# Converting staged pieces of queries, keys and values two steps behind their load, with at most four pieces staged in three steps

## The chip, the cores and the metric

The kernel runs on one core of a Trainium2 chip. The metric is the time of one execution on the device, in microseconds. Before the change the median of three runs is 926.92 us (923.02 to 928.24). TensorE is PE in the rows (PEld its weight loads), VectorE DVE, ScalarE ACT, GpSimd POOL. SyncE, SP, issues nearly all transfers, in the order of its list (SPq in the rows).

## The reference

Attention over 4 batches and 8 heads, 576 positions of 64 numbers each, where each row of scores keeps its 32 largest. Then a dense layer with a maximum over three products, and then a mixture of 8 experts, in which each of the 2304 tokens goes to one:

```python
scores = scale * np.matmul(q, k.transpose(0, 1, 3, 2))
kth = np.partition(scores, -32, axis=-1)[..., -32:-31]
scores = np.where(scores >= kth, scores, -1e9)
attn = softmax(scores); x = attn @ v              # per batch and head
h = np.maximum(np.maximum(x @ w1, x @ w2), x @ w3) @ w_out
expert = argmax(h @ w_gate); p = softmax weight of it
out[expert == e] = p * (np.maximum(h[e] @ ew1[e], 0) @ ew2[e])
```

## The kernel before

All products take float16 pairs: a number is split into a high half and a low half (the rest), and a product is three matmuls. So every operand in float32 must be split, by ACT (high half, scaled) and by DVE (scaled number less high half). For a low half ACT may first write the scaled number to a PSUM buffer (line 740) and DVE subtract from there (line 741); where PSUM buffers are scarce DVE reads the staged number itself (line 734).

The program is written out step by step, each engine's list in the order of the code; no scheduler moves anything. A loop (line 1596) counts steps `t`. One attention tile (128 query rows of a head; two half tiles are paired) enters per step, 144 in all, and its stages lie some steps apart: scores on PE (line 887), evacuation by ACT (894), searches for the 32nd largest on DVE and POOL, exponential on ACT (1046), split of the probabilities on ACT and POOL (1057, 1061), their transposition by a transfer from SP (1066), and product with the values on PE (1080). Between these stand units of the dense layer and of the experts, let in by a credit per step (`run_units`, line 1515): 36 matmuls for a unit of the dense layer, 24 for one of an expert. Where credit is left over and nothing is ready, four filler matmuls are written (1705).

Pieces of queries, keys and values (128 rows of 512 numbers, 256 KB; the last of a batch half of that) come by `preps`, a list of (due step, release step, function, which piece), sorted by due step. In a step at most one released piece begins, or two if the first is due soon. Beginning it (`prep_q`, `prep_k`, `prep_v`, lines 760 to 822) takes one of four staging tiles `st` and issues the load from SP; the function that it returns converts it. Those functions wait in `pend_p`: the conversion stands near the head of the next step, ahead of that step's evacuation on ACT. One step behind the conversion SP issues the transposing transfer of the halves (line 793 for queries), and two steps behind it the copies inside the query tile (797). The weights of one expert use the same staging tiles (`piece`, `half_piece`, lines 1306 and 1319): at most one piece a step, converted two steps behind its load (line 1331).

The 18 tiles of 128 tokens are ranked one after another: the gate product (1195), DVE's choice of an expert, two small matmuls that count tokens per expert (`unit_rank`, 1239 and 1240), and a scatter of the rows to their expert's place (1260). The first expert's tokens are worked on meanwhile, in blocks (slots): a first layer (355) and a second one of four units (366 to 368). When all 18 are ranked, DVE makes the table of the blocks that are left (lines 268 to 331), SP fills gaps (340), issues weight loads that are skipped where the right weights are there already (439, 448) and gathers the rows of the first blocks (427), and `finale` works through the list.

Of the kernel before, what the change touches and what calls it, by code (L numbers as in the profile page):

```python
# [19 lines left out]
def kernel(  # L20
# [43 lines left out]
    WARM, ST = 4, 4  # L64
# [30 lines left out]
    def attempt(ctx, general):  # L95
# [526 lines left out]
        with ExitStack() as p1:  # L622
# [43 lines left out]
            clock = [0]  # L666
# [4 lines left out]
            def after(n, fn):  # L671
                due.setdefault(clock[0] + n, []).append(fn)
# [35 lines left out]
            def stage_tile():  # L708
                if clock[0] < 0:
                    return s_p.tile([P, S], F32, tag="s", name="s")[:, 0:H * D]  # L710
                return st_p.tile([P, H * D], F32, tag="st", name="st")

            def stage_load(src, b, t):
                n = tok_rows(t)
                st = stage_tile().rearrange("p (h d) -> p h d", h=H)
                nc.sync.dma_start(out=st[0:n], in_=src[b, :, t * P:t * P + n, :].rearrange("h p d -> p h d"))
                return st
# [565 lines left out]
            ew, e1, e2, half = [], [], [], [None]  # L1283
# [16 lines left out]
            def piece_ok(i):  # L1300

                if i >= KE:
                    return bool(e2) and i < KE + 2 * KD
                return bool(picked) and clock[0] > picked + 8 and clock[0] > FREE + (0 if i < KE // 2 else L_AV + 1)

            def piece(i):

                st = stage()
                re = nc.sync.value_load(firsti[0:1, 0:1], min_val=0, max_val=NE - 1)
                if i < KE:  # L1310
                    src = ew2[bass.ds(re, 1), i * P:(i + 1) * P, :]
                    hi, lo = (w2e(e, i) for e in range(2))
                else:
                    kk, f = divmod(i - KE, 2)
                    src = ew1[bass.ds(re, 1), kk * P:(kk + 1) * P, f * 512:(f + 1) * 512]
                    hi, lo = (W1e[0][:, e, kk, f * 512:(f + 1) * 512] for e in range(2))
                return split_piece(st, src, hi, lo)

            def half_piece(kk):

                f = half[0]
                st = stage()
                re = nc.sync.value_load(firsti[0:1, 0:1], min_val=0, max_val=NE - 1)
                return split_piece(st, ew1[bass.ds(re, 1), kk * P:(kk + 1) * P, f * 512:(f + 1) * 512],
                                   W1h[0][:, 0, kk], W1h[0][:, 1, kk])
# [197 lines left out]
            for b in range(B):  # L1523
                blocks = [NQ] + list(range(NQ)) if b == B - 1 else list(range(NCH))
                start = b * (NTL // B)
                need = start
                items = []
                for t in range(NCH):
                    items.append((start - 2, start - 24, prep_k, (b, t)))
                for bi, qb in enumerate(blocks):  # L1530
                    items.append((need - 2, need - 6, prep_q, (b, qb)))
                    need += H if qb < NQ else H // 2
                for t in range(NCH):
                    items.append((start + 10, max(start - 12, 2), prep_v, (b, t)))
                preps += items
# [17 lines left out]
            with tc.manual_schedule():  # L1553
# [5 lines left out]
                def begin(it):  # L1559
                    return it[2](*it[3])  # L1560
# [5 lines left out]
                rows = lead[0], lead[1], lead[2], lead[3]  # L1566
                rest_k = lead[4:]
                clock[0] = -8
                pend_p, pend_w = [], []
                pend = [begin(it) for it in rows]  # L1570
                pend.append(begin_w())
                pend.append(begin(rest_k[0]))
# [16 lines left out]
                t = -1  # L1589
# [6 lines left out]
                while second is None or not fin() or len(ranked) < NTT:  # L1596
# [18 lines left out]
                        st_exp(n)  # L1615
                    for go in pend_p:
                        go()
                    pend_p = []
                    avail = [it for it in preps if it[1] <= t]
                    for it in avail[:2 if avail and avail[0][0] - t < 6 else 1]:  # L1620
                        preps.remove(it)
                        pend_p.append(it[2](*it[3]))
                    n = t - L_REST
                    if ok(n):
                        st_rest(n)
# [31 lines left out]
                    pend_w = []  # L1657
                    if wq:

                        for f, a in wq[:2 if t < L_KTH - 2 else 1]:  # L1660
                            wq.pop(0)
                            pend_w.append(f(*a))
                    elif not m_ps and not pend_w and t > 20:
                        p_w.close()
                        m_ps.append(p_m.enter_context(tc.tile_pool(name="mp", bufs=2, side="right")))
                        ew.append(p_m.enter_context(tc.tile_pool(name="ew", bufs=1, side="right")))
                        W1h.append(ew[0].tile([P, 2, KD, 512], F16, name="W1h"))
                    elif piece_ok(len(eld)):
                        after(2, piece(len(eld)))
                        eld.append(t)  # L1670
                    elif len(hld) < KD and half[0] is not None:
                        after(2, half_piece(len(hld)))
                        hld.append(t)
# [94 lines left out]
```

## Time and profile before

| | us |
|---|---|
| median of three runs | 926.92 (923.02 to 928.24) |
| the profiled execution | 929.35 |
| its span, first to last instruction | 927.6 |
| busy: PE / DVE / ACT / POOL | 743.9 / 746.3 / 706.1 / 596.7 |
| mean granted clock of TensorE | 0.966 of 2.4 GHz |

The terms of a sum are made against the profiled execution, and the forecast against the median. A busy share of 76 to 80% over the span is an average over three stretches with different limits, which is why the rows below go by stretch. In a row of a timeline the first two numbers are the start and the duration in us, and the bracket is the engine's idle time ahead of it with what ended it. DMA rows on SP are the time of the issue, not of the transfer.

### The profile page before, as it was taken

How to read it: one execution, taken by the hardware profiler on the slowest of the kernel's cores; microseconds unless marked ns; L12 is line 12 of the kernel's file. 1: busy time of each engine (PE TensorE's matmuls, PEld its weight loads, DVE VectorE, ACT ScalarE, POOL GpSimd, SP SyncE). 2: the span in 40 equal slices, each digit the busy share in tenths (PEclk: the TensorE clock that was granted, in tenths of full speed). 3: DMA queues.
4: the chain of work that ended last, by engine and by line, in shares of the span. 5: the costliest groups of instructions: out<-in, count | busy, mean ns of one | idle time of the engine just before them, and what ended most of it. 6: DMA issues, size and time to landing. Idle time of an engine off the chain costs nothing. (4 is left out here: it accounts for less than half of the span.)

```text
span 927.6 us, 29138 instructions
## 1 busy us (share of the span) xinstructions
PE 743.9 (80%) x10606; PEld 577.4 (62%) x10606; DVE 746.3 (80%) x3108; ACT 706.1 (76%) x1464; POOL 596.7 (64%) x554
## 2 busy tenths in 40 slices
PE   1112367889877899978988899889999999999992
PEld 0001136667665778757777688667987755687871
DVE  5999999999999899998998999998852325477660
ACT  4769899999998899898998999998861231466660
POOL 2547798898988699987877789788982221101110
PEclk9999999999899799998989999989999999999996
DMA  9863968777997798899989798878986568698370
GB/s 229 265 215 72 209 140 164 121 145 124 189 167 158 143 163 169 154 191 178 189 145 171 169 161 137 186 165 147 175 163 115 137 169 309 160 309 224 87 194 16
DMA packets 372165, 155.94 MB, mean 168 GB/s; under 512 B 331931, under 2 KB 348319, under 8 KB 372000
## 3 DMA queue, kind: packets, MB, share of 16 engines
q1 hardware_dynamic: 368128, 143.10, 75.4%
q0 software_dynamic: 3136, 9.46, 3.0%
q8 instruction: 87, 1.43, 0.7%
q10 hardware_dynamic: 736, 1.32, 0.4%
q14 instruction: 78, 0.64, 0.2%
HBM read 76.06 MB, written 16.67 MB: 100 GB/s over the span
## 5 line engine op out<-in xcount | busy, mean ns | idle before, releaser
L355 PEld LDWEIGHTS <-W 128*128 128x128 f16 x4560 | 250.9, 100 | 19.8 <-issue 16.8
L355 PE MATMUL mm<-xT,W 128*128 128x128 f16 x3456 | 215.3, 225 | 15.2 <-DVE vl L741 5.4
L968 POOL TENSOR_TENSOR f<-s,g 128x576 f32<-128x576 f32 x144 | 184.6, 1282 | 45.9 <-ACT g L962 28.2
L1061 POOL TENSOR_TENSOR phl<-e,phl 128x576 f16<-128x576 f32 x144 | 188.1, 1306 | 8.2 <-ACT phl L1057 7.4
L916 DVE MAX8 c<-s 128x8 f32<-128x96 f32 x864 | 175.1, 243 | 12.3 <-ACT s L894 8.7
L887 PEld LDWEIGHTS <-qT 128*128 128x128 f16 (+1 forms) x640 | 56.6, 107 | 191.3 <-issue 157.5
L887 PE MATMUL S<-kt,qT 128*128 128x64 f16 (+3 forms) x320 | 61.5, 342 | 109.2 <-ACT s L894 94.4
L1046 ACT ACTIVATE e<-s,be 128x576 f32<-128x576 f32 x144 | 109.8, 762 | 14.2 <-POOL phl L1061 10.3
L1080 PE MATMUL av<-vh,pt 128*128 128x65 f16 (+3 forms) x1600 | 110.7, 200 | 11.8 <-DVE xn L1129 9.8
L962 ACT ACTIVATE g<-s,bf 128x576 uint16<-128x576 f32 x144 | 111.6, 775 | 5.7
L977 DVE MAX8 vec<-f 128x8 f32<-128x576 f32 x144 | 108.7, 755 | 4.7 <-POOL f L968 1.9
L1040 POOL TENSOR_TENSOR s<-s,g 128x576 f32<-128x576 f32 x72 | 92.8, 1288 | 22.7 <-DVE e L1051 21.6
L1080 PEld LDWEIGHTS <-pt 128*128 128x128 f16 (+3 forms) x2400 | 89.4, 103 | 24.7 <-issue 11.4
L894 ACT ACTIVATE s<-S 128x576 f32<-128x576 f32 x144 | 91.7, 636 | 15.8 <-PE S L887 15.6
L1057 ACT ACTIVATE phl<-e 128x576 f16<-128x576 f32 x144 | 96.2, 668 | 7.9 <-DMA pt<-phl 7.7
L1080 PE MATMUL av<-vl,pt 128*128 128x64 f16 (+3 forms) x800 | 100.2, 197 | 0.0
L1051 DVE SCALAR_TENSOR_TENSOR e<-s,hkth,e 128x576 f32<-128x576 f32 x72 | 87.2, 1211 | 13.1 <-ACT e L1046 12.7
L456 DVE SCALAR_TENSOR_TENSOR W<-st,W 128x1024 f16<-128x1024 f32 x56 | 65.8, 1220 | 36.6 <-ACT W L455 34.5
L887 PE MATMUL S<-kT,qT 128*128 128x512 f16 (+3 forms) x320 | 48.7, 292 | 22.5 <-ACT s L894 22.5
L1164 POOL TENSOR_TENSOR hhl<-a,hhl 128x384 f16<-128x384 f32 x36 | 37.0, 1027 | 33.8 <-ACT hhl L1163 32.5
L455 ACT ACTIVATE W<-st 128x1024 f16<-128x1024 f32 x56 | 55.6, 1046 | 1.8 <-DMA xs<-zrow 1.8
L1037 ACT ACTIVATE g<-s,hkth 128x576 uint16<-128x576 f32 x72 | 54.7, 760 | 0.0
(233 smaller groups left out, 1571.2 us busy)
## 6 DMA issues: line engine op xcount, KB each, us to landing
st<-in_moe_w_dram SPq DMA_DIRECT2D x72, 512.0 KB
st<-in_moe_w_dram SPq DMA_DIRECT2D x28, 256.0 KB
raw<-in_moe_w_dram SPq DMA_DIRECT2D x12, 512.0 KB
st<-in_v_dram SPq DMA_DIRECT2D x16, 256.0 KB
hs<-he SPq DMA_DIRECT2D x16, 256.0 KB
hTe<-hs SPq DMA_DIRECT2D x8, 512.0 KB
st<-in_q_dram SPq DMA_DIRECT2D x15, 256.0 KB
qT<-qT SPq DMA_DIRECT2D x30, 128.0 KB
```

The source lines that it names most:

```text
L355: nc.tensor.matmul(out=ps[:, o * n:(o + 1) * n], lhsT=w(b, kk, c), rhs=x(a, kk), start=(kk == 0 and i == 0), stop=(kk == KD - 1 and i == 2))
L887: nc.tensor.matmul(out=ps[o:o + m, j, 0:(REM if j else NQ * P)], lhsT=qt[:, vv, hh, 0:m], rhs=kr[:, hh] if j else km[:, hh // HG, :, hh % HG],
L894: nc.scalar.activation(out=s, in_=Sps.pop(n).rearrange("p a b -> p (a b)")[:, 0:S], func=ACTF.Copy, scale=DOWN)
L916: nc.vector.max(out=c[:, i * 8:(i + 1) * 8], in_=s[:, i * CW:(i + 1) * CW])
L962: nc.scalar.activation(out=gg[n], in_=Ss[n], func=ACTF.Sign, bias=bf[g][:, i], accum_out=cnt[g][:, i])
L968: let_in(nc.gpsimd.tensor_tensor(out=ff[n], in0=Ss[n], in1=gg.pop(n).bitcast(F16), op=ALU.subtract))
L977: bulk.append(lambda: nc.vector.max(out=y8[g][:, i, 1:9], in_=y))
L1040: let_in(nc.gpsimd.tensor_tensor(out=Ss[n], in0=Ss[n], in1=zz.pop(n).bitcast(F16), op=ALU.subtract))
L1046: nc.scalar.activation(out=e, in_=Ss.pop(n) if early(n) else Ss[n], func=ACTF.Exp, scale=ESC, bias=be[g][:, i])
L1057: nc.scalar.activation(out=ph[:, 0, 0:S], in_=p, func=ACTF.Copy)
L1061: nc.gpsimd.tensor_tensor(out=ph[:, 1, 0:S], in0=p, in1=ph[:, 0, 0:S], op=ALU.subtract)
L1080: nc.tensor.matmul(out=av[o:o + m, i, 0:n], lhsT=t[0:kk, p * NCH + c, o:o + m], rhs=v_rows(x, b, c, hh)[:, 0:n], start=(c == 0 and p == 0 ...
```

## The change

A piece that is begun in step t is converted in step t+2 (`next_p` holds it for a step). Query pieces are released one step earlier, so their conversion stays in its step; pieces of keys and values convert a step later. `staged` notes the step of every staging tile that is taken, by weight pieces too, and a piece begins only while fewer than four were taken in this step and the two before it; until the pool of attention operands is closed this holds for weight pieces also.

```diff
             def stage_tile():
                 if clock[0] < 0:
                     return s_p.tile([P, S], F32, tag="s", name="s")[:, 0:H * D]
+                staged.append(clock[0])
                 return st_p.tile([P, H * D], F32, tag="st", name="st")
+
+            staged = []
+
+            def staging():
+                return sum(c > clock[0] - 3 for c in staged) < ST
...
-                    items.append((need - 2, need - 6, prep_q, (b, qb)))
+                    items.append((need - 2, need - 7, prep_q, (b, qb)))
...
                     for go in pend_p:
                         go()
-                    pend_p = []
+                    pend_p, next_p = next_p, []
                     avail = [it for it in preps if it[1] <= t]
-                    for it in avail[:2 if avail and avail[0][0] - t < 6 else 1]:
+                    for it in avail[:2 if avail and avail[0][0] - t < 7 else 1]:
+                        if not staging():
+                            break
                         preps.remove(it)
-                        pend_p.append(it[2](*it[3]))
+                        next_p.append(it[2](*it[3]))
...
+                    elif not staging() and not e1:
+                        pass
                     elif piece_ok(len(eld)):
```

Lines below the first edit stand six to ten lines lower in the changed kernel: 716 is 722 there, 1239 is 1245.

SP's list around the load of the first full query piece of the last batch (step 105 or 106). Here `qT<-qT` are the copies inside a query tile, `pt<-phl` transposes of probabilities, `xTe<-xs` a gather of an expert's rows, `mte<-xs` its small load. Before:

```order
L797 DMA qT<-qT 64x8x64 x2
L1066 DMA_TRANSPOSE pt<-phl_148 128x10x128
L1371 TENSOR_LOAD eroi
L1371 ISA x2
L1373 ISA
L1373 DMA_TRANSPOSE xTe<-xs 128x8x128
L1375 ISA
L1375 DMA mte<-xs 128x2
L716 DMA st<-in_q_dram 128x8x64
L1066 DMA_TRANSPOSE pt<-phl_149 128x10x128
```

And in the changed kernel:

```order
L722 DMA st<-in_q_dram 128x8x64
L803 DMA qT<-qT 64x8x64 x2
L1441 DMA hs<-he 128x1024
L1193 DMA_TRANSPOSE x2T<-xr 128x8x128
L1072 DMA_TRANSPOSE pt<-phl_148 128x10x128
L1072 DMA_TRANSPOSE pt<-phl_149 128x10x128
L1072 DMA_TRANSPOSE pt<-phl_150 128x10x128
L1377 TENSOR_LOAD eroi
```

The load moved from behind the gather to ahead of the copies; the gather now follows three transposes later.

PE's list around the last of the 18 rankings (`oh` is the choice of an expert, `tri` and `ones` the constant operands; `xTe` and `hTe` are a block's rows for the first and the second layer). Before:

```order
L355 LDWEIGHTS W1e
L355 MATMUL mm<-xTe,W1e 128x128
L1239 LDWEIGHTS tri_70
L1239 MATMUL mm<-oh,tri_70 128x8
L1240 LDWEIGHTS ones_69
L1240 MATMUL mm<-oh,ones_69 128x8
L366 LDWEIGHTS hTe
L366 MATMUL mm<-kt_107,hTe 128x512
```

And in the changed kernel:

```order
L368 LDWEIGHTS hTe
L368 MATMUL mm<-vh_108,hTe 128x512
L1245 LDWEIGHTS tri_70
L1245 MATMUL mm<-oh,tri_70 128x8
L1246 LDWEIGHTS ones_69
L1246 MATMUL mm<-oh,ones_69 128x8
L366 LDWEIGHTS hTe
L366 MATMUL mm<-kt_107,hTe 128x512
```

A block's second layer of 24 matmuls, which stood behind the ranking, now stands ahead of it. Its result goes out by POOL, whose list shows the blocks that follow (`xs<-xr,si` is the scatter of the ranked tile, each `ye` with `mte` one block's result, and with `mt` one of the last stage). Before:

```order
L1209 COPY xr_16330<-tok_68 128x1
L1260 DMA xs_57<-xr_16330,si_16731 19584x514
L400 DMA out_0_dram<-ye_16780,mte_92 2304x512
L400 DMA out_0_dram<-ye_17013,mte_92 2304x512
L400 DMA out_0_dram<-ye_17079,mte_92 2304x512
L400 DMA out_0_dram<-ye_17110,mte_92 2304x512
L400 DMA out_0_dram<-ye_17118,mt_16962 2304x512
```

And in the changed kernel:

```order
L1215 COPY xr_16405<-tok_68 128x1
L400 DMA out_0_dram<-ye_16766,mte_92 2304x512
L1266 DMA xs_57<-xr_16405,si_16804 19584x514
L400 DMA out_0_dram<-ye_16845,mte_92 2304x512
L400 DMA out_0_dram<-ye_17049,mte_92 2304x512
L400 DMA out_0_dram<-ye_17072,mte_92 2304x512
L400 DMA out_0_dram<-ye_17130,mt_17017 2304x512
```

Four blocks followed the last scatter, three do now.

## Rows read from the trace of the kernel before

**Rows 1.** Busy time by stretch: us, busy of each engine, granted clock, DMA share

```profile
core 0: us, PE busy (x) PEld busy (x) DVE busy (x) ACT busy (x) POOL busy (x), PEclk, DMA share, GB/s
100.00:660.00 560.00, 476.60 (x7055) 379.71 (x7055) 524.74 (x2504) 515.34 (x1134) 477.67 (x413) 0.96 0.87 162
660.00:790.00 130.00, 128.85 (x1598) 94.11 (x1596) 57.71 (x228) 50.14 (x99) 51.82 (x59) 1.00 0.71 175
795.95:799.36 3.41, 3.41 (x35) 3.41 (x33) 1.88 (x2) 0.84 (x2) 1.24 (x1) 0.50 0.24 39
...
311.26:318.08 6.82, 5.67 (x54) 5.67 (x54) 5.64 (x28) 5.66 (x15) 3.43 (x3) 0.50 0.85 156
```

**Rows 2.** The evacuations of scores, one a step, line 894

```profile
L894 ACT ACTIVATE s<-S x144: 624/632/673, 15.9 to 658.1; 128x576 f32<-128x576 f32 x144
```

**Rows 3.** Waits from 110 to 660 us: total us, times, longest

```profile
ACT s L894 <- PE S L887: 13.1, 14, 2.9
...
ACT hl L757 <- DMA st<-in_q_dram: 5.9, 4, 3.2
PE mm L355 <- DVE vl L741: 5.4, 2, 3.0
```

**Rows 4.** Timeline of ACT at the four waits for query pieces

```profile
299.66 0.63 ACT L757 ACTIVATE hl<-st 64x512 f16<-64x512 f32 x1 [0.84 <-DMA st<-in_q_dram]
...
424.26 0.63 ACT L757 ACTIVATE hl<-st 128x512 f16<-128x512 f32 x1 [1.24 <-DMA st<-in_q_dram]
...
499.79 0.63 ACT L757 ACTIVATE hl<-st 128x512 f16<-128x512 f32 x1 [3.22 <-DMA st<-in_q_dram]
500.32 0.58 ACT L740 ACTIVATE mm<-st 128x512 f32<-128x512 f32 x1
...
605.88 0.63 ACT L757 ACTIVATE hl<-st 128x512 f16<-128x512 f32 x1 [0.64 <-DMA st<-in_q_dram]
```

**Rows 5.** Timeline of DVE at the same places

```profile
300.80 0.68 DVE L741 TENSOR_TENSOR hl<-mm,hl 64x512 f16<-64x512 f32 x1 [1.03 <-ACT mm L740]
...
425.41 0.69 DVE L741 TENSOR_TENSOR hl<-mm,hl 128x512 f16<-128x512 f32 x1 [1.67 <-ACT mm L740]
...
500.94 0.69 DVE L741 TENSOR_TENSOR hl<-mm,hl 128x512 f16<-128x512 f32 x1 [2.35 <-ACT mm L740]
...
609.21 0.42 DVE L916 MAX8 c<-s 128x8 f32<-128x96 f32 x2 [0.47 <-ACT s L894]
```

**Rows 6.** Timeline of SP's issues ahead of three of these conversions

```profile
294.21 0.69 SPq L716 DMA_DIRECT2D st<-in_q_dram  x1
...
420.39 0.64 SPq L716 DMA_DIRECT2D st<-in_q_dram  x1
...
488.54 2.40 SPq L797 DMA_DIRECT2D qT<-qT  x2
...
493.58 1.26 SPq L1373 DMA_TRANSPOSE xTe<-xs  x1
495.05 1.33 SPq L1375 DMA_DIRECT2D mte<-xs  x1
496.44 0.42 SPq L716 DMA_DIRECT2D st<-in_q_dram  x1
```

**Rows 7.** The filler matmuls: group by line, busy us, mean ns

```profile
L1705 PE MATMUL mm<-WO,ones 128*128 128x512 f16 x52 | 14.3, 400 | 0.1
```

**Rows 8.** Timeline of PE from the last ranking to the last stage

```profile
771.64 0.17 PE L1239 MATMUL mm<-oh,tri 128*128 128x8 f16 x1
...
771.70 0.38 PE L366 MATMUL mm<-kt,hTe 128*128 128x512 f16 x1
...
792.20 0.38 PE L368 MATMUL mm<-vh,hTe 128*128 128x512 f16 x1
794.73 7.15 PE L355 MATMUL ph<-W1h,W1e 128*128 128x128 f16 x96 [2.15 <-DMA W1h<-xs]
```

**Rows 9.** Timeline of DVE and SP between these two points

```profile
771.89 0.17 DVE L1267 TENSOR_TENSOR vec<-mm,base 128x8 f32<-128x8 f32 x1 [1.34 <-PE mm L1240]
...
784.58 0.18 DVE L331 TENSOR_TENSOR chg<-new,live 1x31 int32<-1x31 f32 x1
...
780.61 4.33 SPq L340 DMA_DIRECT2D xs<-zrow  x4
787.39 1.26 SPq L439 DMA_DIRECT2D st<-in_moe_w_dram  x4
788.93 1.66 SPq L448 DMA_DIRECT2D st<-in_moe_w_dram  x4
791.35 1.29 SPq L427 DMA_TRANSPOSE W1h<-xs  x1
```

More of the change, by code (lines that the diff above doesn't have):

```diff
@@ L1568, in attempt @@
                 clock[0] = -8
-                pend_p, pend_w = [], []
+                pend_p, next_p, pend_w = [], [], []
                 pend = [begin(it) for it in rows]
```

## The prediction, made before the changed kernel ran

> **What bounds the kernel now.** I read the kernel in three stretches. In the attention stretch (100 to 660 us) the busy times by stretch show that no engine is free: DVE works 524.7 of 560 us, ACT 515.3, POOL 477.7, PE 476.6 [rows 1]. The 144 evacuations of scores, one a step, run from 15.9 to 658.1 us [rows 2], 4.5 us a step, and a step ends when the last of ACT and DVE is through its list. So a wait is worth something only where ACT and DVE stand still together. From 660 to 790 us the picture is another one: PE works 128.85 of 130 us, DVE 57.7, ACT 50.1 [rows 1]. There PE's instruction count is the time. Behind it comes one more wait of PE, for the rows of the last stage (part 3), and from there to the end the program is the same list in both kernels.
>
> Next, the waits of 110 to 660 us. ACT waits 5.9 us in 4 places for a piece of queries, 13.1 us in 14 places for PE's scores, and PE waits 5.4 us in 2 places because a PSUM buffer that a conversion of values uses is not free yet [rows 3]. The 4 places are the only ones in this stretch where a conversion of queries, keys or values waits for its load. They are 0.84 us at 299.66, 1.24 at 424.26, 3.22 at 499.79 and 0.64 at 605.88 [rows 4].
>
> **Part 1: the load gets a step more.** For queries the load moves one step ahead and the conversion stays where it was (release 7 instead of 6 steps before the need, conversion two steps after the load). For keys and values the load stays and the conversion comes a step later. Work is not added: the two ACT passes of a piece (0.63 and 0.58 us) and DVE's subtraction (0.69 us) only change place [rows 4, 5]. What is taken away is the wait. How much of it comes back is read from DVE beside it: it stood still 1.03, 1.67 and 2.35 us behind the first three, and behind the fourth it went on and lost 0.47 us a little later, waiting for ACT's next evacuation [rows 5]. The smaller of the two engines' idle times at each place is what a step can shrink by: 0.84 + 1.24 + 2.35 + 0.47 = 4.9 us.
>
> Will the load be there in time? At 499.79 it was not late by its own transfer: it was issued at 496.44, when SP came out of a gather of rows and a small load behind it (493.58 + 1.26, then 495.05 + 1.33), and landed 2.9 us after its issue ended [rows 6]. In the changed kernel it stands in SP's list ahead of the copies inside the query tile, which SP reaches today at 488.54, and the gather comes three transposes behind it: SP's order above shows it. That is up to 496.44 - 488.54 = 7.9 us earlier, for a wait of 3.22. At 299.66 and 424.26 the issues stand at 294.21 and 420.39 [rows 6], for waits of about 1 us; a step ahead, 4.5 us, covers both.
>
> The Trainium skill ("DMA: Bandwidth & Descriptors", Anatomy of one DMA) says that a semaphore wait of a DMA is served on the issuing sequencer, before dispatch; so a load written earlier into SP's list still leaves only when all ahead of it have left. The trace agrees where SP's list is dense. Taken strictly it would make this term 0 instead of -4.9 us, and the total 932.6.
>
> The term's ends: 0, if SP is late anyway and the next transposes are what ACT then waits for; about -10, if the looser placing also removes PE's waits for PSUM buffers (5.4 us in 2 places, [rows 3]). I take -4.9, since at the largest place all engines stood still together.
>
> **Part 2: at most four pieces in three steps.** The limit and the later conversions thin out crowded steps: of the eleven conversions of steps 61 to 69 three stood in step 63, now no step has more than two (counted from the code's conditions, step by step). Weight pieces give way, by 1 to 3 steps, and with them the units of PE that use them. The total stays (88 conversions before and now, one more of them with the second ACT pass of 0.58 us, [rows 4]). PE gets 8 more filler matmuls (60 for 52), of 14.3 us / 52 = 0.27 us or less each [rows 7], which stand where nothing else was ready: 0 us, 2.2 at most.
>
> **Part 3: the end of the unit list.** This is what the diff doesn't tell. The later weight pieces shift the order of PE's units, and at the end the last tile's ranking (line 1239) stands elsewhere. Before, four second-layer blocks of 24 matmuls follow it until the last stage begins; now one of them stands ahead of it and three follow (PE's order above). What does the last stage wait for? Follow the chain from the ranking: ranking matmul 771.64, then DVE's table of rows to 784.58 + 0.18, SP's conditional weight loads from 787.39 to 790.6, the first gather of rows at 791.35, PE's first matmul at 794.73 [rows 8, 9]. That is 794.73 - 771.64 = 23.1 us. PE had work for 96 matmuls behind the ranking: from 771.70 to 792.20 are 95 intervals, 0.216 us each, so 20.7 us [rows 8], and then it stood 2.15 us. So the chain already sets the end, and everything behind the ranking is fixed: 927.6 - 771.64 = 156 us. A block that moves ahead of the ranking therefore costs its full 24 x 0.216 = 5.2 us, since PE has no idle time ahead of it in that stretch (128.85 of 130 us busy, [rows 1]); PE's wait at the last stage grows from 2.15 to about 7.4 us. Bounds: 3, if the chain is shorter because the row scatter lands sooner (pads could not start before 780.61, [rows 9], but the table alone reaches 784.76, so little is to be had); 5.6 if other small waits join.
>
> Behind that wait the granted clock is 0.50 from 795.95 to 799.36, which is 1.2 GHz, and PE is busy all the time [rows 1]: 1.7 us lost today. Around PE's longest wait for a PSUM buffer of values, 3.0 us [rows 3], the low clock lasted from 311.26 to 318.08 [rows 1], so a longer wait may cost 0 to 1.7 us more; I take 0.5, nearer to the row of this very place.
>
> The Trainium skill ("TensorE: Matmul & The Clock Gate", What's actually happening) calls the low clock the resting state that activity releases. Both stretches agree with it; by it the longer wait would give the upper end, 1.7 us in place of 0.5, and a sum 1.2 us higher.
>
> **The sum.** The profiled execution took 929.35 us (span 927.6), 2.4 us more than the median of the three runs, 926.92. 929.35 - 4.9 + 0 + 5.2 + 0.5 = 930.15; against the median that is 926.92 + 0.8 = 927.7 us. The two main terms cancel.
>
> **Rivals.**
> Full price, no gain (slower): the load's wait goes, but ACT and DVE give nothing back, because SP, which works its list off in order, is what the steps at 299.66, 424.26 and 499.79 wait for: the load leaves earlier there, the transposes behind it leave later, and ACT stands at the next of these instead. Then only the tail counts: 926.92 + 5.2 + 0.5 = 932.6, and 933.8 with the low clock at its upper end. It decides as soon as the attention stretch gets shorter by under 1 us, for then the total is over 931.6. For it: ACT's larger wait is for PE's scores, 13.1 us, not for loads [rows 3]. Against it: at 499.79 DVE stood 2.35 us too.
> Gain beyond the waits (faster): thinner steps also free PSUM buffers sooner, so PE's two waits of 5.4 us and part of ACT's 13.1 us for scores go as well [rows 3]. Then the attention stretch gives 10 to 11 us, and the total is 926.92 - 10.5 + 5.7 = 922.1.
> No price at the end: the chain behind the ranking shrinks by what PE lacks, since ACT and SP reach their lists sooner. Then 926.92 - 4.9 = 922.0. Against it: DVE's table ran without a wait for PE and took from 771.89 to 784.76 [rows 9], and it stays.
> The change doesn't do what it says: a wait at the same four conversions, of another cause (the tile for the halves, two buffers, or a full SP list). Its time is that of the first rival.
>
> **How the numbers follow.** Both terms as sized: 0.47, at 927.7, with 924 to 931 as its own range. Full price, no gain: 0.27. Gain beyond the waits: 0.15. No price at the end: 0.11. A measurement of this kernel can tell about 0.5% from no change, 4.6 us, so faster is below 922.3 and slower above 931.6. Faster: a good half of the two lower cases (0.26) and a little of the first, 0.19. Slower: most of the 0.27 and a little of the first, 0.28. Within: the rest, 0.53. The range takes in the lower cases to 921.5 and the upper one to 933.8.
>
> **What would show it.** Right: no wait of a query conversion for its load over 0.5 us; the last evacuation of scores (line 894, now 900) 4 to 6 us earlier than 658.1 [rows 2]; the last ranking matmul within 2 us of 771.64; then 72 matmuls and a wait of PE of 7 to 8 us for the rows. Wrong in the first term: that evacuation is within 1 us of today's. Wrong in the last: PE's wait at the last stage stays near 2 us, or the chain from ranking to last stage is not 23 us. Anything before step 20 or behind the first last-stage matmul that moves by over 2 us would lie outside this account.

## The result, and the profile after

The changed kernel is slower: 932.38 us, the median of 8 executions (931.14 to 938.38), against 926.59 for the kernel before in the same rounds. The ratio is 1.0080, with a 95% interval of 1.0058 to 1.0102. A second time, with 23 executions of the kernel before beside it, it was 934.10 against 924.78, 1.0095 (1.0075 to 1.0115). The forecast was 927.7, no change that can be told; the time lies in its range and at the number of its first rival, 932.6.

| us | before, the profile of the forecast | before, a second profile | after | after, a second profile |
|---|---|---|---|---|
| the profiled execution | 929.35 | 926.41 | 932.33 | 932.01 |
| span | 927.6 | 924.7 | 930.6 | 930.3 |
| last evacuation of scores | 658.1 | 653.8 | 658.0 | 657.6 |
| last ranking | 771.64 | 767.5 | 774.51 | 774.4 |
| first matmul of the last stage | 794.73 | 790.07 | 795.78 | 795.6 |

The second column is the one that the forecast didn't have. The same program, instruction for instruction, came to its last evacuation 4.3 us sooner. The profile that the forecast was read from was an unusually long execution in just the stretch from which its gain was read; between it and the profile after, the attention stretch looks unchanged, and against the second profile it got 4 us longer (a third profile of the same program up to there, the late ranking below, ends the stretch at 654.1).

The kernel after, busy times by stretch, answering [rows 1], and the group of the evacuations, answering [rows 2]:

```profile
100.00:660.00 560.00, 477.87 (x7091) 380.72 (x7091) 526.63 (x2495) 512.95 (x1133) 476.25 (x412) 0.97 0.85 161
660.00:790.00 130.00, 130.00 (x1581) 94.22 (x1581) 56.83 (x234) 49.22 (x99) 53.14 (x59) 1.00 0.73 178
794.60:801.43 6.83, 5.64 (x54) 5.64 (x54) 6.59 (x6) 4.34 (x6) 0.00 (x0) 0.50 0.50 115
...
L900 ACT ACTIVATE s<-S x144: 623/632/672, 16.5 to 658.0; 128x576 f32<-128x576 f32 x144
```

The second profile of the kernel before, the same group and the waits of 110 to 660 us. Three of the four waits for query pieces are still there, with 5.3 us, beside a last evacuation at 653.8:

```profile
L894 ACT ACTIVATE s<-S x144: 624/632/672, 16.1 to 653.8; 128x576 f32<-128x576 f32 x144
...
ACT s L894 <- PE S L887: 11.5, 10, 2.7
...
ACT hl L757 <- DMA st<-in_q_dram: 5.3, 3, 3.7
ACT phl L1057 <- DMA pt<-phl: 3.5, 4, 1.5
```

The waits of the kernel after, answering [rows 3]. The row of the query pieces is gone. The row of the transposed probabilities, 4.4 us in 4 places in the forecast's profile and 3.5 in 4 in the second, has become the second longest of ACT:

```profile
ACT s L900 <- PE S L893: 11.4, 11, 2.1
ACT phl L1063 <- DMA pt<-phl: 9.9, 6, 3.9
ACT e L1052 <- POOL phl L1067: 6.5, 8, 1.2
```

Where the longest of the four waits stood, in the step that ends at 500.7, ACT and SP of the kernel after read as follows (answering [rows 4] and [rows 6]):

```profile
498.31 0.68 ACT L1063 ACTIVATE phl<-e 128x576 f16<-128x576 f32 x1 [3.87 <-DMA pt<-phl]
498.90 0.61 ACT L763 ACTIVATE hl<-st 128x512 f16<-128x512 f32 x1
...
487.31 1.74 SPq L722 DMA_DIRECT2D st<-in_q_dram  x1
489.11 1.34 SPq L803 DMA_DIRECT2D qT<-qT  x2
490.56 0.57 SPq L1441 DMA_DIRECT2D hs<-he  x1
491.23 1.64 SPq L1193 DMA_TRANSPOSE x2T<-xr  x1
493.33 5.00 SPq L1072 DMA_TRANSPOSE pt<-phl  x3
```

The load left at 487.31 instead of 496.44, and the conversion at 498.90 waits for nothing. The instruction ahead of it now waits 3.87 us for three transposes that SP issued in one run from 493.33 to 498.33. The wait changed its name and kept its length: from 487.31 to 498.33 SP issued one transfer after another, with no gap of over 0.5 us.

The end of the list, answering [rows 8] and [rows 9]: TensorE around the last ranking and at the last stage, then DVE's table and SP's issues between them.

```profile
774.30 0.38 PE L368 MATMUL mm<-vh,hTe 128*128 128x512 f16 x1
774.51 0.17 PE L1245 MATMUL mm<-oh,tri 128*128 128x8 f16 x1
...
789.89 0.38 PE L368 MATMUL mm<-vh,hTe 128*128 128x512 f16 x1
795.78 1.44 PE L355 MATMUL ph<-W1h,W1e 128*128 128x128 f16 x12 [5.52 <-DMA W1h<-xs]
...
774.76 0.17 DVE L1273 TENSOR_TENSOR vec<-mm,base 128x8 f32<-128x8 f32 x1 [3.84 <-PE mm L1246]
...
787.01 0.18 DVE L331 TENSOR_TENSOR chg<-new,live 1x31 int32<-1x31 f32 x1
...
780.52 4.64 SPq L340 DMA_DIRECT2D xs<-zrow  x4
788.75 1.26 SPq L439 DMA_DIRECT2D st<-in_moe_w_dram  x4
790.29 1.21 SPq L448 DMA_DIRECT2D st<-in_moe_w_dram  x4
792.58 1.28 SPq L427 DMA_TRANSPOSE W1h<-xs  x1
```

TensorE waits 5.52 us for the rows instead of 2.15, and the chain from the ranking to the last stage is 795.78 - 774.51 = 21.3 us instead of 23.1. From the ranking to the end it is 930.6 - 774.51 = 156.1 us, as before (156.0).

### The profile page after: what moved, and what is told of

Its sections match the earlier page's. It is cut to its first block, busy times and chain, and to the rows that moved or that the text cites. A ratio compares the mean times of both kernels' runs of the same rounds, so it can differ in the third digit from the quotient of the medians.

```text
span 930.6 us, 29171 instructions
## 1 busy us (share of the span) xinstructions
PE 745.4 (80%) x10614; PEld 578.7 (62%) x10614; DVE 749.8 (81%) x3108; ACT 705.1 (76%) x1465; POOL 597.4 (64%) x554
## 5 line engine op out<-in xcount | busy, mean ns | idle before, releaser
L1170 POOL TENSOR_TENSOR hhl<-a,hhl 128x384 f16<-128x384 f32 x36 | 34.9, 971 | 34.7 <-ACT hhl L1169 34.6
L355 PEld LDWEIGHTS <-W1e 128*128 128x128 f16 x864 | 51.6, 101 | 7.6 <-issue 5.8
```

The source lines that it names most:

```text
L355: nc.tensor.matmul(out=ps[:, o * n:(o + 1) * n], lhsT=w(b, kk, c), rhs=x(a, kk), start=(kk == 0 and i == 0), stop=(kk == KD - 1 and i == 2))
```

## The experiments

All kernels ran beside the kernel before on the same chip. The last three columns are from one profiled execution each.

| kernel | us | before | ratio (95%) | last evacuation | last ranking | last stage |
|---|---|---|---|---|---|---|
| queries only | 923.21 | 925.21 | 0.9971 (0.9947 to 0.9995) | 652.9 | 766.1 | 788.7 |
| the same, repeated | 923.13 | 923.45 | 0.9999 (0.9982 to 1.0016) | 651.4 | 764.7 | 786.8 |
| no limit | 924.16 | 925.00 | 0.9992 (0.9977 to 1.0007) | 652.6 | 766.2 | 788.1 |
| limit only | 930.31 | 925.21 | 1.0059 (1.0036 to 1.0083) | 654.7 | 768.8 | 791.6 |
| the same, repeated | 930.77 | 925.00 | 1.0055 (1.0041 to 1.0069) | 657.9 | 772.0 | 794.9 |
| limit not on weights | 923.61 | 923.45 | 1.0008 (0.9987 to 1.0029) | 653.5 | 766.8 | 789.6 |
| limit on weights only | 929.70 | 923.45 | 1.0073 (1.0047 to 1.0098) | 657.4 | 774.0 | 795.3 |
| before, late ranking | 929.62 | 925.21 | 1.0058 (1.0035 to 1.0081) | 654.1 | 772.0 | 792.8 |
| after, early ranking | 933.15 | 925.21 | 1.0078 (1.0049 to 1.0107) | 659.4 | 771.1 | 795.8 |
| after, early ranking, its scatter ahead | 926.36 | 925.00 | 1.0018 (0.9999 to 1.0037) | 658.3 | 770.9 | 793.2 |
| the same, repeated | 927.62 | 924.78 | 1.0029 (1.0014 to 1.0044) | 655.8 | 767.4 | 789.6 |
| queries only, five blocks behind the ranking | 929.82 | 925.00 | 1.0041 (1.0024 to 1.0058) | 655.0 | 769.4 | 795.3 |
| after, repeated | 934.10 | 924.78 | 1.0095 (1.0075 to 1.0115) | 657.6 | 774.4 | 795.6 |
| before, repeated | 924.38 | 924.78 | 0.9988 (0.9969 to 1.0007) | 653.8 | 767.5 | 790.1 |

### The queries alone

```diff
-                    items.append((need - 2, need - 6, prep_q, (b, qb)))
+                    items.append((need - 2, need - 7, prep_q, (b, qb)))
...
-                    pend_p = []
+                    pend_p, next_p = next_p, []
...
-                    for it in avail[:2 if avail and avail[0][0] - t < 6 else 1]:
+                    for it in avail[:2 if avail and avail[0][0] - t < 7 else 1]:
                         preps.remove(it)
-                        pend_p.append(it[2](*it[3]))
+                        (next_p if it[2] is prep_q else pend_p).append(it[2](*it[3]))
```

> The kernel before, in which only the pieces of queries are loaded one step earlier and converted two steps behind their load; keys and values stay one step behind, there is no limit of four, and the order of the units on TensorE is that of the kernel before, so the tail is the same. Theory 1 (the forecast's first term): the four waits of ScalarE for query pieces were lost time; the last evacuation of scores comes some 4.9 us earlier and the time is about 921.7 us. Theory 2 (SP's queue sets those steps): the waits go, others of up to 3.9 us for the transposed probabilities come in their place, the last evacuation stays within 1 us of 658.1 and the time within 1.5 us of 926.6.

Measured: 923.21 us, 0.9971, which is 2.0 us by the medians and 2.7 by the ratio (0.5 to 4.9 by its interval), between the two theories. The repeat, the same program:

> The kernel before with only the pieces of queries converted two steps behind their load, the same program as the first run of that kind, whose interval, 0.9947 to 0.9995, just leaves 1 out. Theory 1 (the four waits for query pieces are worth half of the 4.9 us that the forecast gave them): 922 to 924 us, 1.5 to 3 below the kernel before. Theory 2 (they are worth nothing, and the first run was a lucky round): within 1 us of the kernel before.

Measured: 0.9999, theory 2 against the kernel before beside it. TensorE's list is that of the kernel before, and ACT's waits read (first run):

```profile
ACT s L894 <- PE S L887: 9.1, 9, 2.2
ACT e L1046 <- POOL phl L1061: 9.1, 12, 1.2
ACT phl L1057 <- DMA pt<-phl: 5.5, 6, 1.6
...
ACT vh L820 <- DMA st<-in_v_dram: 1.5, 3, 0.8
```

SP's issues of the same run around the largest place:

```profile
486.89 1.37 SPq L716 DMA_DIRECT2D st<-in_q_dram  x1
488.36 1.67 SPq L797 DMA_DIRECT2D qT<-qT  x2
490.14 1.87 SPq L1066 DMA_TRANSPOSE pt<-phl  x1
492.85 1.26 SPq L1373 DMA_TRANSPOSE xTe<-xs  x1
494.32 0.59 SPq L1375 DMA_DIRECT2D mte<-xs  x1
495.03 1.35 SPq L1066 DMA_TRANSPOSE pt<-phl  x1
```

The four waits are gone in both runs and no transpose is waited for longer than 1.6 us: here the load left early, and the transposes behind it stand one by one between other transfers, not three in a run. Yet the last evacuation is only 0.9 and 2.4 us ahead of 653.8, and the medians gained 2.0 and 0.3 us. Between the evacuations of steps 103 and 107 the two runs gained 4.1 and 3.9 us against the second profile of before, so the longest wait did come back there. The first run had lost 2.3 us by step 103, and gave back 0.9 more from step 107 to the last. Profiles of one program differ by as much between these steps, so what took the rest isn't shown. By the medians and ratios the gain of the forecast's first term is between nothing and about half of it.

### Without the limit, and the limit by parts

The changed kernel without both conditions on `staging()`:

```diff
                     for it in avail[:2 if avail and avail[0][0] - t < 7 else 1]:
-                        if not staging():
-                            break
                         preps.remove(it)
...
-                    elif not staging() and not e1:
-                        pass
```

> The changed kernel without the limit of four: queries, keys and values are all converted two steps behind their load, queries loaded a step earlier; the last tile's ranking is again followed by four second-layer blocks. Theory 1 (the limit is what costs: alone it took the kernel before from 925.2 to 930.3 us, and the later conversion of queries alone gave 2 us back): the time is 922 to 924 us, 8 to 10 below the changed kernel. Theory 2 (keys and values converted a step later lose what the queries win): 925 us or above, while the last evacuation of scores comes at 655 us or later.

Measured: 924.16 us, 0.9992, nearer to theory 1. TensorE's list is then that of the kernel before, row by row. Converting all pieces two steps behind costs nothing that can be seen in the time and brings nothing. In its profile the waits for query pieces are gone as well, but two others have come: of 3.6 us at 418 us, for a tile of halves that the transfer of a key piece (`kT<-hl`) still reads, and of 3.0 us at 491, for a transpose of probabilities (the row gives total, times, longest):

```profile
ACT phl L1057 <- DMA pt<-phl: 4.9, 4, 3.0
ACT hl L757 <- DMA kT<-hl: 3.6, 1, 3.6
```

So the loss comes with the limit. The kernel before with the limit alone:

```diff
+                staged.append(clock[0])
                 return st_p.tile([P, H * D], F32, tag="st", name="st")
...
+                        if not staging():
+                            break
...
+                    elif not staging() and not e1:
+                        pass
```

> The kernel before with only the limit of four pieces in three steps; every piece is still converted one step behind its load, and four blocks follow the last ranking as before. Theory 1 (the forecast's second term): the limit costs nothing and the time stays within 1 us of 926.6. Theory 2 (the limit moves units of the experts among the attention steps and so costs there): the last evacuation of scores comes 1 to 4 us later than 658.1 and the time is 928 to 931 us.

Measured: 930.31, theory 2 by the time; but the profile is of the shortest of its executions (925.78) and has its last evacuation at 654.7, so it showed no place. The repeat:

> The kernel before with only the limit of four, the same program as the first run of that kind, for another profile and more times: those of the first spread in two groups, 925.8 to 928.3 and 930.3 to 934.6 us, and its profile fell in the lower one. Theory 1 (the limit costs in the attention steps): the median is again 929 to 931.5 us, and a profile of the upper group has its last evacuation of scores 3 us or more later than 654.7 us. Theory 2 (the upper group was a disturbance of those rounds): the median is within 1.5 us of the kernel before.

Measured: 930.77, theory 1, and this profile ends its attention stretch at 657.9. Which of the limit's two conditions is it? First the changed kernel without the second one (the weights):

```diff
-                    elif not staging() and not e1:
-                        pass
```

> The changed kernel, in which the limit of four holds back only pieces of queries, keys and values; the pieces of the experts' weights are again loaded without regard to it. The experts' first-layer blocks are then given out in the steps of the kernel before (the fourth of the second group stands at step 80 behind an idle step again, not right behind another), and the end of the list is that of the kernel before. Theory 1 (the limit costs by moving the loads of the experts' weights, and with them the units): 922.5 to 925.5 us, no wait of TensorE of over 2 us for the first layer's result between steps 80 and 83. Theory 2 (the pieces of queries, keys and values held back are what costs): 929 to 933 us.

Measured: 923.61, 1.0008. Then without the first one (queries, keys, values):

```diff
                     for it in avail[:2 if avail and avail[0][0] - t < 7 else 1]:
-                        if not staging():
-                            break
                         preps.remove(it)
```

> The changed kernel, in which the limit holds back only the pieces of the experts' weights; queries, keys and values are loaded when they come due. The order of the units from step 70 to the end is that of the changed kernel, with three blocks behind the last ranking. Theory 1 (the weights' pieces held back are what costs): 930 to 934 us, with the 3 to 4.5 us wait of TensorE at step 82 and the last stage at 794 us or later. Theory 2 (the other pieces): 922.5 to 926 us.

Measured: 929.70, 1.0073. Theory 1 in both (the second one 0.3 us below its range). The whole loss hangs on the two lines that let the pieces of the experts' weights give way. They shift these pieces by up to four steps, the first-layer blocks that use them by up to five (the blocks begun at steps 66, 69, 72 and 80 are begun at 70, 73, 77 and 80), and so the units behind them.

One place where this costs can be read. At 377 to 386 us the block begun at step 77, whose units stand at 79, is now followed at step 80 by the next one, with units at 82. TensorE's row of the changed kernel and of the one with the limit on weights only, then DVE's of the changed kernel (line 1057 is the masking, which sets to zero what is below the 32nd largest):

```profile
381.68 1.54 PE L355 MATMUL mm<-xT,W 128*128 128x128 f16 x13 [3.28 <-DVE he L1437]
...
381.85 1.37 PE L355 MATMUL mm<-xT,W 128*128 128x128 f16 x12 [4.50 <-DVE he L1437]
```

```profile
378.67 2.25 DVE L1057 SCALAR_TENSOR_TENSOR e<-s,hkth,e 128x576 f32<-128x576 f32 x1 [1.11 <-ACT e L1052]
380.84 0.20 DVE L941 MAX8 T<-c 128x8 f32<-128x48 f32 x1
380.96 0.67 DVE L1437 SCALAR_TENSOR_TENSOR he<-mm,he 128x512 f16<-128x512 f32 x1
```

TensorE stands 3.3 to 4.5 us because the PSUM tile that it wants is emptied by DVE behind a masking of 2.25 us. The masking is as long at this step in the kernel before (2.18 us in its second profile), but TensorE doesn't wait for it there. From step 79 to 83 the evacuations of all eight profiles of kernels that limit the weights fall 3.8 to 5.5 us behind those of the kernel before; with the limit not on weights, TensorE has no wait of over 1.0 us there. That this collision is the cause of the whole loss in the attention steps is not shown: these kernels stand 0.4 us behind to 3.0 ahead of the second profile of before at step 79, and 1.0 to 5.6 us behind it at the last evacuation, so other steps take and give too.

### The end of the unit list

The kernel before, whose last ranking is held back by a block:

```diff
                 for j in jobs:
...
+                    if j.u == NU1 + 3 and posted[0] == NTT - 1 and slots[6].u < 8:
+                        continue
```

> The kernel before, in which the last tile's ranking is held back until the second layer of slot 6 is written, so that three second-layer blocks (72 matmuls) follow the last ranking instead of four; nothing else is changed. Theory 1 (the chain from the last ranking to the last stage sets the end): the last ranking comes some 5 us later, TensorE waits 6 to 8 us instead of 2.15 ahead of the last stage, and the time is 3 to 6 us above the kernel before, 929.5 to 932.5 us. Theory 2 (the chain shortens by as much as the ranking comes later, since what stretches it is the work beside it): the time stays within 1.5 us of 926.6.

Measured: 929.62, 1.0058, 4.4 us by medians and 5.4 by the ratio: theory 1. The ranking stands 117.9 us behind the last evacuation (113.5 and 113.7 in the profiles of before), and TensorE waits 5.03 us at the last stage:

```profile
792.77 4.53 PE L355 MATMUL ph<-W1h,W1e 128*128 128x128 f16 x41 [5.03 <-DMA W1h<-xs]
```

The time behaves as forecast, the wait only by half: the chain is 20.8 us here and was 23.1.

The reverse, the changed kernel with the ranking a block earlier:

```diff
                 for s in sorted(slots, key=lambda s: s.u >= 4):
...
+                    if s.u >= 4 and s.i >= 6 and jobs:
+                        continue
```

> The changed kernel, in which the second layers of slots 6 and up are held until the last ranking is given out, so that four blocks (96 matmuls) follow the last ranking as in the kernel before. Theory 1 (the whole loss of the change lies at the end of the unit list): the last ranking comes some 5 us earlier than in the changed kernel, the wait ahead of the last stage falls from 5.5 to 1 to 3 us, and the time falls by 3 to 5.8 us to 926.6 to 929.4 us. Theory 2 (the loss lies in the attention stretch, where waits for the transposes took the place of waits for loads): the time stays within 1.5 us of 932.4.

Measured: 933.15, nothing regained, and theory 2 seemed to hold. But the profile has the ranking 3.4 us earlier, and the last stage at 795.81 as in the changed kernel, so the chain had grown to 24.7 us. POOL's timeline of this kernel tells why:

```profile
777.49 0.98 POOL L400 DMA_INDIRECT out_dram<-ye,mte  x1 [13.12 <-DVE rw L286]
778.78 0.98 POOL L1266 DMA_INDIRECT xs<-xr,si  x1 [0.31 <-issue]
```

The scatter of the ranked rows stands in POOL's list behind the output of a block that TensorE computes after the ranking; its indices were ready at 773.6, and it left 5.2 us later. So the hold was lengthened by one step:

```diff
-                    if s.u >= 4 and s.i >= 6 and jobs:
+                    if s.u >= 4 and s.i >= 6 and posted[0] < NTT:
```

> The changed kernel, in which the second layers of slots 6 and up are held until the step after the last ranking, so that four blocks follow the ranking and its scatter on GpSimd's queue is issued ahead of slot 6's output instead of behind it (in the run that held them only until the ranking itself, the scatter came 7.7 us after the last ranking matmul, against 2.65 in the kernel before). Theory 1 (half or more of the loss lies in the order of the units at the end): the scatter comes within 3 us of the ranking, the last stage starts at 790 to 793 us instead of 795.8, and the time is 926.5 to 929.5 us. Theory 2 (the loss lies ahead of it, in what the limit does to the attention steps): 931 to 933.5 us, the last stage no more than 1 us earlier.

Measured: 926.36, 1.0018, theory 1. The lists of TensorE, DVE and SP of these two kernels are the same, row by row; one entry of POOL changed places, and one output on ACT:

```profile
774.09 0.99 POOL L1266 DMA_INDIRECT xs<-xr,si  x1 [10.15 <-DVE lv L270]
777.25 0.98 POOL L400 DMA_INDIRECT out_dram<-ye,mte  x1 [2.17 <-ACT ye L399]
```

By the medians of this run and of its repeat that is worth 5.5 to 6.8 us, by the ratios 4.5 to 5.5. The profiles show 2.4 us of it, in the chain from the ranking to the last stage (24.7 us, then 22.3 and 22.2); the rest is not located. The shares of the end and of the attention steps were then still open, so this kernel, the changed one and the one before ran again side by side:

> The changed kernel with the second layers of slots 6 and up held until the step after the last ranking, the same program as the first run of that kind (926.4 us; its profiled execution, 930.0, was among its slowest), beside the changed kernel and the kernel before in the same call. Theory 1 (most of the loss lies behind the attention steps, in how late the last ranking comes): the median is 926 to 928 us, 4 to 6 below the changed kernel. Theory 2 (most lies in the attention steps, where the profiles of the limited kernels end 3 to 5 us later): 929 to 931.5 us, no more than 3 below the changed kernel.

> The changed kernel itself, for more times beside its variant with the early ranking and for a second profile. Both theories expect 1.006 to 1.010 of the kernel before. Theory 1 (the loss lies behind the attention steps): a profile has its last evacuation of scores at 653 to 656 us and the last stage still at 794 us or later. Theory 2 (it lies in them): the last evacuation again at 657 to 659 us, with the wait of TensorE of 3 to 4.5 us at step 82.

> The kernel before itself, for a second profile: the one that the forecast was read from took 929.35 us, 2 to 4 us above the medians of this kernel. Theory 1 (the forecast's profile was a slow execution in the attention steps, and the four waits of ScalarE for query pieces belong to it only in part): the last evacuation of scores comes at 652 to 655 us instead of 658.1, with at least three of the four waits still there. Theory 2 (658 us is usual): 657 to 659 us.

Measured: 927.62, 934.10 and 924.38. By the medians the variant is 6.5 us faster than the changed kernel, theory 1. The second profile of the changed kernel has its last evacuation at 657.6 and a wait of 4.49 us at step 82, theory 2; that of before has its at 653.8, theory 1. Both readings fit together when the stretch from the last evacuation to the end is taken from the profiles: 269.5 and 270.9 us before, 272.6 and 272.7 after, but 270.0 and 266.6 in the variant. The variant doesn't only undo the loss at the end, it is some 2 us better there than the kernel before, and about 3 us worse in the attention steps (657.1, the mean of its two profiles, against 654.0, that of the second profile of before and of the kernel with the late ranking alone, whose program is the same up to there). So by the profiles the changed kernel loses about 4 us in the attention steps and 2.5 at the end, of the 7.4 to 8.8 that the ratios tell; 1 to 2.5 us are not located, and how they are shared stays open. The 2.5 is the weaker figure: the same stretch took 266.3 to 271.8 us in the eight profiles of kernels whose end of the list is that of before. Up to the first matmul of the last stage it spreads less (135.4 to 137.0 us in these eight), and there the changed kernel's 137.8 and 138.0 are 1.2 to 1.7 us more than the 136.6 and 136.3 of the two profiles of before.

A try to do better than both held back a block more, on top of the queries alone:

```diff
+                    if s.u >= 4 and s.i >= 5 and jobs:
+                        continue
```

> The kernel with only the queries' later conversion (923.2 us), in which the second layers of slots 5 and up are held until the last ranking is given out: five blocks (120 matmuls, about 26 us at 0.22 us each) follow it, more than the chain of 22 to 23 us to the last stage. Theory 1 (TensorE's wait ahead of the last stage and the low clock behind it are the price of a chain without cover): the wait of 1.6 us is gone, the low clock behind it too, and the time falls by 1.5 to 3.5 us to 920 to 921.7 us. Theory 2 (the work held back is only moved, and something else is late next): 922.5 to 924 us.

Measured: 929.82, 1.0041, against both theories. The wait at the last stage is gone, as theory 1 had it; the low clock that it wanted to save is not there in the profile of the queries alone to begin with. But ahead of the ranking TensorE now waits for an expert's rows:

```profile
761.77 7.79 PE L355 MATMUL mm<-xTe,W1e 128*128 128x128 f16 x96 [3.93 <-DMA xTe<-xs]
```

and the last stage starts 140.3 us behind the last evacuation instead of 136.3 in the second profile of before. In the queries alone, where the block held back stands ahead of the ranking, this wait is 0.6 us. No kernel of this study beats the kernel before beyond doubt.

## Why the prediction was wrong

**What bounds the kernel.** The views were read rightly, from an execution that was 4.3 us longer in the attention stretch than a second one of the same program. Working the sum out against the median can't mend that when a term is read from just that stretch.

**Part 1 failed.** The four waits for query pieces went, as forecast. What came back was 0 to 2.7 us, not 4.9: the repeated run of the queries alone gave 0.9971 and 0.9999. The step that failed is "the smaller of the two engines' idle times at each place is what a step can shrink by", added up over four places and taken as the gain of the whole stretch. With the queries alone the largest place did give back 4 us, and the last evacuation still came only 0.9 and 2.4 us sooner; where the rest went stays open. In the changed kernel ACT's wait at the largest place didn't even shrink: the text followed the load forward in SP's list and priced the 7.9 us that it wins, and put no price on the transpose of rows and the three transposes of probabilities that its order showed behind the load. The text had named this as its lower end, and did not take it because all engines had stood still at that place. The load's move by itself doesn't do this, since with the queries alone no transpose is waited for longer than 1.6 us; without the limit, with keys and values converted later too, one is waited for 3.0 us. The Trainium skill's rule ("DMA: Bandwidth & Descriptors", Anatomy of one DMA), by which a semaphore wait of a DMA is served on the issuing sequencer before dispatch, was weighed there with a total of 932.6. POOL's scatter above agrees: its indices were ready at 773.6, and it left at 778.78, behind an output that still waited for its rows. At SP's largest place the trace shows the order of issue, 3.87 us behind three transposes in a row, with no gap of over 0.5 us that such a wait could fill.

**Part 2 failed.** "0 us, 2.2 at most" priced the added filler matmuls alone: it saw that the weight pieces give way "and with them the units of PE that use them", found the total unchanged, and so put no price on where they land. (The pieces moved by up to four steps, not by 1 to 3.) The limit, of all the change's parts, is what costs: 1.0008 without its condition on the weights, 1.0073 with that condition alone. In the attention steps the largest loss that was found is a collision of two expert blocks with one masking on DVE, a wait of TensorE of 3.3 to 4.5 us at step 82. The limit alone, with pieces converted one step behind, cost 5 to 5.5 us although its end of the list was that of before; with the later conversion and four blocks behind the ranking it cost 1.7 to 2.7. About 2 of these 3 us are the better end of that variant; whether the later conversion takes back the rest isn't settled.

**Part 3 held in kind, and in size by the late ranking alone.** The moved block was sized 5.2 us and 0.5 for the clock; done alone, it measured 4.4 to 5.4. In the changed kernel the profiles show 1.2 to 1.7 us up to the last stage. Its details were off. The chain that was to stay at 23.1 us was 21.3 (20.8 when done alone), because the pads started 3.6 us behind the scatter's issue, not 6.3: SP issued them from 780.52 after a scatter at 776.97, where it had been 780.61 after one at 774.29. Of these 2.7 us 1.8 are left in the chain. The bound of 3 us named this case. So TensorE's wait grew to 5.52 us, not 7.4. The ranking itself was to come within 2 us of 771.64, 4.9 sooner by part 1 and 5.2 later by the block. With nothing from part 1 it came 2.9 later; of the 2.3 that lack, 1.2 are idle time of TensorE ahead of it that was used up (130.00 of 130 us busy, 128.85 before). The granted clock at the last stage was 0.50 for 6.83 us after the wait of 5.52, where it had been 0.50 for 3.41 after one of 2.15; with TensorE busy 5.64 us of it instead of 3.41, that is 1.1 us more by the prediction's reckoning, not 0.5. But what follows can't be put down to it: in the second profile of before the clock stays at full speed there, and last stage to end is 134.6 us, in the first one 132.9.

**The rivals.** "Full price, no gain" had the time, 932.6, and its point of decision, an attention stretch that shortens by under 1 us: 658.1 to 658.0. Its mechanism, SP's order, is shown at the largest wait. That the number fits is in part luck: the rival lacked the limit's price in the attention steps, about 4 us, which the long profile hid, and its price of the end, 5.7 us, is more than the profiles show there. "Gain beyond the waits" fell: ACT's 13.1 us for scores became 11.4, which is what the second profile of before has too (11.5), and the stretch got no shorter. "No price at the end" fell with the late ranking alone. Of what the text named as signs, "wrong in the first term: that evacuation is within 1 us of today's" is what happened, and so is a chain from ranking to last stage that is not 23 us.

## What to carry to other kernels

Moving one entry of an in-order queue forward can end its wait, as with the queries alone, or only rename it, as in the changed kernel; write down what stands behind it in the new order and price that too. Idle time that two engines share is read at one step, and says little about the whole stretch. In a schedule that is worked out from conditions, a small condition on one kind of load can move everything that hangs on it, so compare the whole order on each engine, and above all the last dependent chain: one scatter behind the wrong output cost 4.5 to 6.8 us here. Before a gain of a few us is read from a stretch, look at a second profile of the same kernel.

## What the runs showed of the hardware that I had not expected

Two executions of one program stood 0.4 us apart at step 47 of the attention steps, 1.3 at step 67, 3.4 at step 95, 1.8 at step 115 and 4.3 at the last one. A difference of a few us between two profiles of two programs says little by itself there.

The scatter of one tile's rows was waited for longer, the closer SP's last weight load stood ahead of it. With 0.9 to 1.3 us between that load's issue and the scatter's, SP's pads started 6.0 to 6.7 us behind the scatter (six profiles), with 2.3 to 2.6 us 5.2 and 5.5, and with 5.0 to 9.3 us 3.1 to 3.6 (seven profiles). The sixteenth profile, of five blocks behind the ranking, doesn't count, since SP issued another load between scatter and pads there. That the transfers of the loads are what the scatter waits behind is an argument; it was not tested by itself.
